# Holding back prefetch loads behind score blocks, and four x transposes by PE instead of DMA

## The chip, the cores and the metric

One core of a Trainium2 chip runs the whole kernel. The metric is the device time of one execution in microseconds (us); lower is better. Before the change it was 352.68 us (median of 3 runs, 351.48 to 353.09).

Engines, by what they do in this kernel: PE multiplies matrices, DVE (VectorE) and ACT (ScalarE) work on vectors, POOL issues the loads from device memory, SP issues the DMA transposes and the moves of v inside SBUF, where the kernel keeps its tiles. DMA engines carry out these transfers; the profile counts 16 of them for the core. PE's results go to PSUM (`ps` in the profile). The **landing** of a transfer is its time from issue to completion.

## The reference, cut to what matters

```python
# q, k, v: (8 batches, 8 heads, 576 positions, 64); window 64, causal
scores = q @ k^T / 8;  scores outside 0 <= i - j < 64 are masked
attn   = softmax(scores);  x = (attn @ v) as (4608 tokens, 512)
out    = (silu(x @ w_gate) * (x @ w_val)) @ w_out     # 512 -> 1536 -> 512
```

## The kernel before

The 4608 tokens are handled as 36 **chunks** n of 128 tokens (attention) and 9 **blocks** c of 512 tokens, four chunks each (feed-forward). The steps have these names:

- `load(n)`: POOL issues the loads of k, q and v of a chunk, float32 to bf16, into rings of 4 (k, q) and 10 (v) buffers.
- `T(n, "k")`, `T(n, "q")`: SP issues DMA transposes of k and q. `T8(n)` is both, and the shift of v by 64 rows (`shift_v`).
- `S(n)`: PE's scores, ACT's exponentials, DVE's mask. `AV(n)`: PE multiplies by v, DVE divides; the result is `xb`, 128 x 512 in bf16.
- `X(n)`: xb is transposed into `xT`, either by a DMA transpose from SP or by PE, with a copy out of PSUM. SP's lines in the traces stand in program order too, so an `X(n)` can stand behind a `T8` that waits for its load (chunk 11's x in the kernel before: ready at 83.75 us, issued at 85.94, behind T8(13)).
- `F(c, f)`: gate and value products of a block (8 matmuls), `O(c, u)`: output product (12 matmuls).

Each engine is given its own steps in program order. F(c, 0) needs the x of **all four** chunks of the block: F(2, 0) needs X(8) to X(11).

```python
    def load(self, n, what="kqv"):
        ...
                self.g.op("pool", lambda e, d=d, a=a: e.dma_start(d, a), writes=ks, dma=True)

    def T(self, n, x):                       # i = n % 4: the ring of k and q
        ...
        self.g.op("sp", lambda e: e.dma_start_transpose(d, src[:, :]), reads=[(x + "n", i, j) for j in range(2)],
                  writes=wk, dma=True)

    def X(self, n, eng="sp"):
        ...
        if eng == "sp":
            g.op("sp", lambda e: e.dma_start_transpose(xo, xb[:, :]), reads=xk, writes=[("xT", it, u)], dma=True)
            return
        bank, bk = self.bank("a")            # one of three PSUM banks, shared with S and AV
        ...                                  # 4 PE transposes, then a copy by eng ("act" or "dve")

    def build(self):
        ...
        for n in (8, 9, 10, 11):
            self.load(n)
        for n in (8, 9, 10):
            self.T8(n)
            self.load(n + 4)
        ...                                  # S, AV, X of 6 and 7; F(1, f) in halves
        F1(0, 1); self.O(0, 0); self.S(8)
        F1(2, 3); self.AV(8); self.X(8); self.T8(11); self.load(15)
        F1(4); self.O(0, 1); self.S(9)
        F1(5, 6); self.AV(9); self.X(9); self.T8(12); self.load(16)
        F1(7); self.S(10); self.O(0, 2); self.AV(10); self.X(10)
        self.F(1, 8); self.S(11); self.T8(13); self.load(17)
        self.F(1, 9); self.AV(11); self.X(11)
        self.F(1, 10); self.O(0, 3); self.S(12); self.T8(14); self.load(18)
        self.F(1, 11)
        for c in range(2, NFC):
            for u in range(4):
                n = 4 * c + u + 4
                self.F(c, 3 * u)
                self.AV(n)
                self.T(n + 3, "k")
                self.X(n)
                self.T(n + 3, "q")
                self.shift_v(n + 3)
                self.load(n + 7)
                self.F(c, 3 * u + 1)
                self.S(n + 1)
                ...                          # O(c - 1, u), F(c, 3 * u + 2)
```

(The calls of `build` are put several to a line here.)

The softmax here doesn't subtract the row's maximum and nothing guards it: scores larger than these inputs give would overflow.

Of the kernel before, what the change touches and what calls it, by code (L numbers as in the profile page):

```python
# [5 lines left out]
ALU = mybir.AluOpType  # L6

B, H, S, D = 8, 8, 576, 64
DM, DFF = H * D, 1536
T = B * S  # L10
# [139 lines left out]
class _Kernel:  # L150
# [70 lines left out]
    def segs(self, t0, size):  # L221
        r = 0
        while r < size:
            b, s = divmod(t0 + r, S)
            L = min(size - r, S - s)
            yield r, b, s, L
            r += L
# [44 lines left out]
            out=m[:, :], in_=m[:, :], compare_op=ALU.not_equal, fill=1.0, base=0,  # L272
            pattern=[[-1, 128]], channel_multiplier=1), writes=[key])

    def load(self, n, what="kqv"):
        if n >= NCH:
            return
        parts = list(self.segs(128 * n, 128))
        for x in what:
            src = {"k": self.k, "q": self.q, "v": self.v}[x]  # L280
            if x == "v":
                dst, nm, i = self.va[n % self.NV], "va", n % self.NV
            else:
                i = n % self.NQ
                dst = (self.kn if x == "k" else self.qn)[i][:, :].rearrange("p (h d) -> p h d", h=H)
                nm = x + "n"
            for j, (r, b, s, L) in enumerate(parts):
                d = dst[r:r + L, :, 0:64]
                a = src[b, :, s:s + L, :].rearrange("h p d -> p h d")
                ks = [(nm, i, j)] if len(parts) > 1 else [(nm, i, 0), (nm, i, 1)]  # L290
                self.g.op("pool", lambda e, d=d, a=a: e.dma_start(d, a), writes=ks, dma=True)  # L291

    def shift_v(self, n, eng="sp"):
        if n >= NCH:
# [48 lines left out]
    def S(self, n, bias=False):  # L343
        if n >= NCH:
            return
        g = self.g
        ip, iz = n % self.NP, n % self.NZ
        pt = self.pt[ip]
        bx = [self.bank("a"), self.bank("a")]
        sv = [b[0][:, :].rearrange("p (w c q) -> p w c q", w=2, c=4) for b in bx]  # L350
        nm = self.nmask[:, :].rearrange("p (a q) -> p a q", a=4)[:, self.var(n)]
        nm = nm.unsqueeze(2).to_broadcast([128, 2, 4, 64])

        def pe(e):
            if bias:
                for p in range(2):
                    e.matmul(sv[p], self.ident[:, :], nm, start=True, stop=False)  # L357
            for w in range(2):
                k0 = 128 * n + 64 * w
                for c in range(4):  # L360
                    for p in range(2):
                        ps = slice(64 * p, 64 * p + 64)
                        r = e.matmul(sv[p][:, w, c], self.kT[ps, c, k0:k0 + 128],  # L363
                                     self.qT[ps, c, self.qs(n, 64 * w, 64 * w + 64)],
                                     start=not bias, stop=not bias or (w == 1 and c == 3))
            return r

        rd = [("kT", m, b) for m in (n - 1, n) for b in range(2)] + [("qT", iz, b) for b in range(2)]
        rd += ["nmask", "ident"] if bias else []
        g.op("pe", pe, reads=rd, writes=[b[1] for b in bx])  # L370
        m = self.mask[:, :].rearrange("p (a q) -> p a q", a=4)[:, self.var(n)]
        m = m.unsqueeze(2).to_broadcast([128, 2, 4, 64])
        for p in range(2):
            po = pt[:, p::2, :].rearrange("p h (x q) -> p x h q", x=3)[:, 0:3:2]
            pk = ("pt", ip, p)
            g.op("act", lambda e, po=po, p=p: e.activation(po, sv[p], ACTF.Exp, scale=SCALE), reads=[bx[p][1]], writes=[pk])  # L376
            if not bias:
                g.op("dve", lambda e, po=po: e.tensor_tensor(po, po, m, ALU.mult), reads=[pk, "mask"], writes=[pk])  # L378
# [269 lines left out]
    def build(self):  # L648
        self.opening()
        self.Tpe(4, ("dve", "act"))  # L650
        self.F(0, 6)
        self.S(4)
        self.F(0, 7)
        self.AV(4)
        self.Tpe(5, ("dve", "act"))
        self.F(0, 8)
        self.X(4, "act")
        self.S(5)
        self.F(0, 9)
        self.AV(5)  # L660
        self.F(0, 10)
        self.X(5, "act")
        self.F(0, 11)
        self.Tpe(6, ("dve", "act"))
        self.Tpe(7, ("dve", "act"))
        for n in (8, 9, 10, 11):
            self.load(n)
        for n in (8, 9, 10):
            self.T8(n)
            self.load(n + 4)  # L670
        F1 = lambda *fs: [self.F(1, f, 0, 256) for f in fs]
        F1(0)
        self.S(6)
        F1(1, 2)
        self.AV(6)
        F1(3)
        self.S(7)
        F1(4)
        self.X(6, "act")
        F1(5)  # L680
        self.AV(7)
        F1(6, 7)
        self.X(7, "act")
        self.banks("a", [5, 6, 7])
        self.banks("o", [4])
        F1 = lambda *fs: [self.F(1, f, 256, 512) for f in fs]
        F1(0, 1)
        self.O(0, 0)
        self.S(8)
        F1(2, 3)  # L690
        self.AV(8)
        self.X(8)
        self.T8(11)
        self.load(15)
        F1(4)
        self.O(0, 1)
        self.S(9)
        F1(5, 6)
        self.AV(9)
        self.X(9)  # L700
        self.T8(12)
        self.load(16)
        F1(7)
        self.S(10)
        self.O(0, 2)
        self.AV(10)
        self.X(10)
        self.F(1, 8)
        self.S(11)
        self.T8(13)  # L710
        self.load(17)
        self.F(1, 9)
        self.AV(11)
        self.X(11)
        self.F(1, 10)
        self.O(0, 3)
        self.S(12)
        self.T8(14)
        self.load(18)
        self.F(1, 11)  # L720
        for c in range(2, NFC):
            for u in range(4):
# [4 lines that stand above are left out]
                self.X(n)  # L727
                self.T(n + 3, "q")
                self.shift_v(n + 3)
                self.load(n + 7)  # L730
                self.F(c, 3 * u + 1)
                self.S(n + 1)
                late = c == NFC - 1 and u == 3
                if not late:
                    self.O(c - 1, u)
                self.F(c, 3 * u + 2)
                if late:
                    self.O(c - 1, u)
        self.banks("o", [0, 1, 2, 3])
        for u in range(3):  # L740
            self.O(NFC - 1, u)
        self.O_last(NFC - 1, 3)
        self.g.emit()
# [42 lines left out]
```

## Time and profile before

| | before |
|---|---|
| time, median (range) | 352.68 us (351.48 to 353.09) |
| span of the profiled execution | 348.9 us (time 350.69) |
| PE busy | 330.9 us |
| PE gap before block 2 | 6.05 us, ends at 94.46 us |
| iteration in steady state | 8.70 us |

First, lines of the profile's page of the kernel before: the busy line, then rows of 40 slices of 8.7 us. A digit is tenths; PEclk is the clock granted to PE.

```profile
span 348.9 us, 6788 instructions
PE 330.9 (95%) x2689; PEld 171.5 (49%) x2689; DVE 222.5 (64%) x495; ACT 136.1 (39%) x248; POOL 111.3 (32%) x139
...
PE   7889998989399999999999999999999999999996
...
PEclk9999999999699999999999999999999999999999
DMA  9999999999999999999999999999934421100012
```

PE is full except in the opening and in one slice, the eleventh (87 to 96 us): busy 3, clock 6. The DMA engines are full from the start to about 250 us. A long row of nines says that transfers are under way nearly all the time, not that PE waits for them: from 100 to 250 us PE is busy for 150.00 of 150 us under them. What PE waits for is in the waits. Here they are for PE of the kernel before, 60 to 100 us (us in total, times, longest):

```profile
PE ps L500 <- issue: 6.0, 1, 6.0
PE ps L363 <- DVE uu L519: 1.2, 1, 1.2
PE ps L363 <- DVE xb L403: 0.7, 1, 0.7
```

"issue" means that the profile shows no releaser. The timeline says what came next. The PE lines of the kernel before around the gap (start, length, then idle time before it in brackets; L363 scores, L500 feed-forward; x4 or x16 is the number of matmuls in a line):

```profile
79.19 0.41 PE L363 MATMUL ps<-qT,kT 64*128 64x64 bf16 x16 [1.21 <-DVE uu L519]
...
87.39 1.03 PE L500 MATMUL ps<-xT,Wv 128*128 128x512 bf16 x4
94.46 1.86 PE L500 MATMUL ps<-xT,Wg 128*128 128x512 bf16 x4 [6.05 <-issue]
96.12 1.70 PE L500 MATMUL ps<-xT,Wv 128*128 128x512 bf16 x4
```

The group at 94.46 us is F(2, 0). Its x of chunk 11 was issued by SP at 85.94 us. And the group runs at about half speed: 1.66 us from start to start instead of 0.86, at a granted clock of 0.53 (94.46 to 97.70 us). The last view is the DMA issues of the kernel before between 60 and 95 us (count, KB each, median us from issue to landing):

```profile
qn<-in_q_dram POOLq DMA_DIRECT2D x5, 128.0 KB, 11.6
va<-in_v_dram POOLq DMA_DIRECT2D x5, 128.0 KB, 12.3
kn<-in_k_dram POOLq DMA_DIRECT2D x4, 128.0 KB, 10.7
...
kT<-kn SPq DMA_TRANSPOSE x6, 8.2
qT<-qn SPq DMA_TRANSPOSE x5, 9.1
xT<-xb SPq DMA_TRANSPOSE x4, 8.4
```

The x transpose of chunk 11, issued at 85.94 us, itself landed 8.4 us later, so at 94.3 us: that is PE's gap. Later in the same kernel (150 to 200 us) the same transpose lands in 4.1 us.

### The profile page before, as it was taken

The page shows a single profiled execution, that of the slowest core. Times are in us where ns is not written, and L with a number is a line of the kernel's source. Part 1 is how long each engine was busy: PE and PEld are TensorE (multiplying, and loading weights), DVE is VectorE, ACT ScalarE, POOL GpSimd, SP SyncE. Part 2 cuts the span into 40 slices and gives each one's busy share as a digit, 9 for nine tenths or more (in the row PEclk, how much of TensorE's full clock was granted, in tenths as well). Part 3 has the DMA queues.
Part 4 walks back from the last instruction along what each step waited for, and adds up shares of the span by engine and source line. Part 5 has one row for each costly group of instructions (what it writes and reads, how often), then busy time and mean ns, then how long its engine had stood idle before and what let it go on. Part 6 is the DMA issues. An engine that isn't in the chain of part 4 may idle for free.

```text
span 348.9 us, 6788 instructions
## 1 busy us (share of the span) xinstructions
PE 330.9 (95%) x2689; PEld 171.5 (49%) x2689; DVE 222.5 (64%) x495; ACT 136.1 (39%) x248; POOL 111.3 (32%) x139
## 2 busy tenths in 40 slices
PE   7889998989399999999999999999999999999996
PEld 3557575644144444444444444444444444444444
DVE  8788987475256666666666666666666666655520
ACT  3545463433134443333333333333333333232321
POOL 8999562634343334233233334232100000000000
PEclk9999999999699999999999999999999999999999
DMA  9999999999999999999999999999934421100012
GB/s 174 173 183 190 183 200 164 175 154 178 178 165 150 159 141 141 133 143 147 134 147 133 148 136 146 142 141 119 147 94 96 107 47 46 57 30 30 32 50 102
DMA packets 176543, 45.46 MB, mean 130 GB/s; under 512 B 160064, under 2 KB 172032, under 8 KB 176512
## 3 DMA queue, kind: packets, MB, share of 16 engines
q0 software_dynamic: 118368, 18.36, 77.5%
q1 hardware_dynamic: 51920, 16.84, 28.2%
q10 hardware_dynamic: 6224, 9.83, 8.1%
q8 instruction: 21, 0.34, 0.4%
q14 instruction: 10, 0.08, 0.1%
HBM read 37.75 MB, written 9.44 MB: 135 GB/s over the span
## 4 chain that ended last, share of the span: by engine, by line
PE 86%; DVE 6%; ACT 3%; issue 3%; DMA 1%; ACTq 0%
PE ps L500 49%; PE ps L546 27%; PE ps L363 3%; PE ps L393 2%; PE ps L394 2%; DVE uu L519 2%; ACT pt L376 2%; DMA hT<-in_k_dram 1%; DVE xb L403 1%; DVE hT L522 1%; PE ps L568 1%; ACT sig L511 1%; ACT ost L551 1%; PE ps L476 1%; PE ps L357 0%
## 5 line engine op out<-in xcount | busy, mean ns | idle before, releaser
L519 DVE SCALAR_TENSOR_TENSOR uu<-sig,ps 128x512 bf16<-128x512 bf16 (+1 forms) x122 | 75.9, 622 | 90.9 <-ACT sig L511 90.2
L500 PE MATMUL ps<-xT,Wg 128*128 128x512 bf16 (+1 forms) x488 | 114.3, 357 | 8.2 <-issue 6.0
L500 PE MATMUL ps<-xT,Wv 128*128 128x512 bf16 (+1 forms) x488 | 114.0, 356 | 0.2 <-DMA Wv<-in_moe_w_val_dram 0.2
L511 ACT ACTIVATE sig<-ps 128x512 bf16<-128x512 f32 (+1 forms) x122 | 66.8, 550 | 107.6 <-PE ps L500 107.5
L546 PE MATMUL ps<-Wo,hT 128*128 128x512 bf16 x420 | 96.1, 380 | 0.0
L522 DVE SCALAR_TENSOR_TENSOR hT<-uu,ps 128x512 bf16<-128x512 bf16 (+1 forms) x122 | 76.3, 625 | 4.4 <-PE ps L500 0.2
L500 PEld LDWEIGHTS ps<-xT,Wv 128*128 128x128 bf16 x488 | 47.5, 98 | 47.2 <-issue 1.1
L500 PEld LDWEIGHTS ps<-xT,Wg 128*128 128x128 bf16 x488 | 44.3, 98 | 47.3 <-issue 7.1
L546 PEld LDWEIGHTS ps<-Wo,hT 128*128 128x128 bf16 x420 | 39.1, 98 | 44.7
L291 POOL DMA_DIRECT2D qn<-in_q_dram x38 | 33.2, 878 | 79.6 <-DMA qT<-qn 79.5
L291 POOL DMA_DIRECT2D kn<-in_k_dram x38 | 33.3, 878 | 53.2 <-DMA kT<-kn 47.2
L376 ACT ACTIVATE pt<-ps 128x512 bf16<-128x512 f32 x72 | 39.0, 595 | 22.4 <-PE ps L363 21.2
L551 ACT ACTIVATE ost<-ps 128x512 f32<-128x512 f32 x35 | 20.9, 597 | 67.0 <-PE ps L546 67.0
L291 POOL DMA_DIRECT2D va<-in_v_dram x40 | 35.4, 890 | 0.2 <-issue 0.2
L403 DVE TENSOR_TENSOR xb<-ps,rc 128x256 bf16<-128x256 f32 x72 | 30.5, 424 | 2.5
L378 DVE TENSOR_TENSOR pt<-pt,mask 128x512 bf16<-128x512 bf16 x64 | 24.8, 419 | 10.1 <-ACT pt L376 9.6
L393 PE MATMUL ps<-vb,pt 128*128 128x65 bf16 x288 | 22.8, 193 | 0.1
L394 PE MATMUL ps<-va,pt 128*128 128x65 bf16 x288 | 22.9, 194 | 0.0
L393 PEld LDWEIGHTS ps<-vb,pt 128*128 128x128 bf16 x288 | 20.2, 98 | 4.5 <-DVE pt L378 0.9
L394 PEld LDWEIGHTS ps<-va,pt 128*128 128x128 bf16 x288 | 19.0, 97 | 3.4
L363 PEld LDWEIGHTS ps<-qT,kT 64*128 64x128 bf16 x576 | 10.4, 95 | 16.3 <-DVE rc L400 9.3
L363 PE MATMUL ps<-qT,kT 64*128 64x64 bf16 x576 | 14.7, 191 | 1.9 <-DVE uu L519 1.2
(47 smaller groups left out, 84.7 us busy)
## 6 DMA issues: line engine op xcount, KB each, us to landing
out_dram<-ost ACTq DMA_DIRECT2D x35, 256.0 KB, 2.9
vb<-va SPq DMA_DIRECT2D x63, 80.0 KB, 3.3
va<-in_v_dram POOLq DMA_DIRECT2D x32, 128.0 KB, 5.3
kn<-in_k_dram POOLq DMA_DIRECT2D x30, 128.0 KB, 5.5
qn<-in_q_dram POOLq DMA_DIRECT2D x30, 128.0 KB, 5.3
Wo<-in_moe_w_out_dram POOLq DMA_DIRECT2D x2, 768.0 KB, 15.2
Wg<-in_moe_w_gate_dram POOLq DMA_DIRECT2D x4, 256.0 KB, 7.3
Wv<-in_moe_w_val_dram POOLq DMA_DIRECT2D x4, 256.0 KB, 7.9
```

Source lines behind the costliest of these rows:

```text
L291: self.g.op("pool", lambda e, d=d, a=a: e.dma_start(d, a), writes=ks, dma=True)
L363: r = e.matmul(sv[p][:, w, c], self.kT[ps, c, k0:k0 + 128], self.qT[ps, c, self.qs(n, 64 * w, 64 * w + 64)], start=not bias, stop=not bias ...
L376: g.op("act", lambda e, po=po, p=p: e.activation(po, sv[p], ACTF.Exp, scale=SCALE), reads=[bx[p][1]], writes=[pk])
L378: g.op("dve", lambda e, po=po: e.tensor_tensor(po, po, m, ALU.mult), reads=[pk, "mask"], writes=[pk])
L393: e.matmul(av[:, j, :], pt[:, h, 0:128], vb[:, h, 0:65], start=True, stop=False)
L394: r = e.matmul(av[:, j, :], pt[:, h, 64:192], va[:, h, 0:65], start=False, stop=True)
L403: g.op("dve", lambda e, xo=xo, av=av, rb=rb: e.tensor_tensor(xo, av[:, :, 0:64], rb, ALU.mult), reads=[bk, ("rc", ir)], writes=[("xb", ix, ...
L500: r = e.matmul(bank[:, lo:hi], W[:, kk, f * 128:f * 128 + 128], xT[:, kk, lo:hi], start=(kk == 0), stop=(kk == NK - 1))
L511: self.g.op("act", lambda e: e.activation(sig[:, lo:hi], G[:, lo:hi], ACTF.Tanh, scale=0.5), reads=[gk], writes=[("sig", i)])
L519: g.op("dve", lambda e: e.scalar_tensor_tensor(uu[:, lo:hi], sig[:, lo:hi], 1.0, G[:, lo:hi], ALU.add, ALU.mult), reads=[("sig", i), gk], ...
L522: g.op("dve", lambda e: e.scalar_tensor_tensor(hT[:, f, lo:hi], uu[:, lo:hi], 0.5, V[:, lo:hi], ALU.mult, ALU.mult), reads=[("uu", i), vk] ...
L546: r = e.matmul(OB[:, :], hT[:, f, 128 * u:128 * u + 128], self.Wo[:, f, :], start=(f == 0), stop=(f == NF - 1))
```

## The change

The intent, as the code shows it: keep the early loads of later chunks off the DMA while block 2's x is being made, and keep that x off the DMA altogether.

1. Gate: `load(12)` and later wait for a score step, S(n - 4), or S(n - 5) from chunk 16 on. In the loop this also makes the load one chunk shallower: n + 6 after S(n + 1), instead of n + 7.
2. `T8(11)` moves forward, right behind T8(10).
3. X(8) to X(11) go by PE, with the copy by ACT.

```diff
-    def load(self, n, what="kqv"):
+    def load(self, n, what="kqv", after=None):
+        gate = [] if after is None else [("S", after)]
...
-                self.g.op("pool", lambda e, d=d, a=a: e.dma_start(d, a), writes=ks, dma=True)
+                self.g.op("pool", lambda e, d=d, a=a: e.dma_start(d, a), reads=gate, writes=ks, dma=True)
...                                    (S(n) also writes the key ("S", n))
-        for n in (8, 9, 10):
+        for n in (8, 9, 10, 11):
             self.T8(n)
-            self.load(n + 4)
...
         self.S(8)
+        self.load(12, after=8)
         F1(2, 3)
         self.AV(8)
-        self.X(8)
-        self.T8(11)
-        self.load(15)
         F1(4)
         self.O(0, 1)
+        self.X(8, "act")
         self.S(9)
+        self.load(13, after=9)
+        self.T8(12)
         F1(5, 6)
         self.AV(9)
-        self.X(9)
-        self.T8(12)
-        self.load(16)
         F1(7)
+        self.X(9, "act")
         self.S(10)
+        self.load(14, after=10)
+        self.T8(13)
         self.O(0, 2)
         self.AV(10)
-        self.X(10)
         self.F(1, 8)
+        self.X(10, "act")
         self.S(11)
-        self.T8(13)
-        self.load(17)
+        self.load(15, after=11)
         self.F(1, 9)
         self.AV(11)
-        self.X(11)
+        self.T8(14)
         self.F(1, 10)
+        self.X(11, "act")
+        self.S(12)
+        self.load(16, after=11)
+        self.load(17, after=12)
         self.O(0, 3)
-        self.S(12)
-        self.T8(14)
-        self.load(18)
...                                    (in the loop)
-                self.load(n + 7)
                 self.F(c, 3 * u + 1)
                 self.S(n + 1)
+                self.load(n + 6, after=n + 1)
```

More of the change, by code (lines that the diff above doesn't have):

```diff
@@ L369, in S @@
         rd += ["nmask", "ident"] if bias else []
-        g.op("pe", pe, reads=rd, writes=[b[1] for b in bx])
+        g.op("pe", pe, reads=rd, writes=[b[1] for b in bx] + [("S", n)])
         m = self.mask[:, :].rearrange("p (a q) -> p a q", a=4)[:, self.var(n)]
```

## The prediction

> **What bounds it now.** PE is busy 330.9 of 348.9 us. From about 100 us to 300 us the timeline repeats one 8.70 us iteration without a PE gap: three feed-forward blocks (1.73 us each), an output block (2.60), attention (about 0.9). The change can't shorten that. The loss to recover lies in 60 to 98 us:
>
> - The waits of PE show one gap of 6.05 us ending at 94.46 us, labelled "issue". The next matmul is the first feed-forward of token block 2, which needs the x of chunks 8 to 11. Chunk 11's x transpose was issued at 85.94 us, and this line's landings take 6.9 to 9.8 us (60 to 95 us), against about 4 later: about 94.4.
> - The two groups after it take 3.2 us instead of 1.73; granted clock 0.66 in 90 to 100 us. [...] Cost 1.5 us.
> - The scores of chunk 11 start 1.2 us late (79.19). By the pool queue's waits chunk 11's qT landed near there.
>
> All are long DMA landings: between 60 and 95 us the k, q, v loads land in 10 to 13 us (whole run: 5.3), the kT, qT, xT transposes in 8 to 9. [...] early loads of chunks 12 to 18 delay the urgent transposes.
>
> **What the change does.** It holds the loads to one chunk per score block, moves chunk 11's transposes ahead of them, and takes four x transposes off the DMA.
>
> Removed from the critical path: 6.05 + 1.5 + 1.2 = 8.8 us.
>
> Added to it: four PE transposes of x, 0.22 to 0.25 us each: 0.9 us. Each has an ACT copy (0.60 us) ahead of the next exponentials, and takes one of three attention PSUM banks; PE already waits 0.7 us for one at 72.67. I estimate 1.0 us of small new waits there.
>
> Steady state: a load is one chunk later, still over two iterations (17 us) ahead of use. But k, q and v now start together just as the x transpose is issued; before, usually only k met it, with landings of 3.6 to 4.6 us. The x of each block's last chunk has about 4.5 us until PE needs it (134.98 to 139.46). I allow 1 us in all for four such boundaries.
>
> Net: 8.8 - 0.9 - 1.0 - 1.0 = 5.9 us off the span, 343.0 us. The profiled run (350.69) is 2 us below the unprofiled median (352.68); part may be the same DMA wait, varying by run, so I subtract 7.5 from the median.
>
> **Prediction: 345.2 us, range 342.5 to 349.0.** Faster by over 2%: 0.54; within 2%: 0.44; slower: 0.02.
>
> **What would show it right.** The 6 us gap leaves PE's waits; no granted clock near 0.66 at 90 us; block 2's first feed-forward starts near 89 us; transposes land in about 4 us or less between 60 and 95 us; POOL waits on PE's scores instead of kT and qT; iterations stay 8.70 us.
>
> **What would make it wrong.** Gaps of 0.5 to 2 us before the first feed-forward of blocks 3 to 6 (late x, colliding with gated loads) would eat up to 6 us. Bank and ACT waits around AV(9) to AV(11) of over 2 us in sum. A gap only halved, because its cause is not DMA crowding.

The 1.5 us for the clock is read from the trace. That early loads delay the transposes was the author's estimate, from loads that landed in 10 to 13 us here against 5.3 over the whole run; e9 below tests it.

## The result, and the profile after

The kernel after took 343.75 us (median of 4 runs, 343.43 to 344.10) against 352.31 us of before (4 runs): ratio 0.9758, 95% interval 0.973 to 0.9785, faster by 2.4%. Ratios are the mean time of one kernel's fast runs over that of the other's in the same rounds, so not quite the ratio of the medians quoted. The profiled execution took 343.43 us, span 341.6 us.

The same lines of the page, of the kernel after:

```profile
span 341.6 us, 6841 instructions
PE 330.3 (97%) x2705; PEld 172.2 (50%) x2705; DVE 222.5 (65%) x495; ACT 138.3 (40%) x252; POOL 111.8 (33%) x139
...
PE   7889998989999999999999999999999999999996
...
PEclk9999999999999999999999999999999999999999
```

The hole in PE and the slow clock are gone. PE's waits of the kernel after, 60 to 100 us, and PE's lines where block 2 begins (at 88.66 us), with the one larger wait that is new (L423 is the PE transpose of x, here chunk 9's):

```profile
PE ps L423 <- DVE xb L404: 1.6, 2, 1.3
PE ps L394 <- DVE pt L379: 0.2, 1, 0.2
```

```profile
73.09 0.40 PE L423 MATMUL ps<-ident,xb 128*128 128x128 bf16 x4 [1.28 <-DVE xb L404]
...
87.80 1.03 PE L501 MATMUL ps<-xT,Wv 128*128 128x512 bf16 x4
88.66 1.03 PE L501 MATMUL ps<-xT,Wg 128*128 128x512 bf16 x4
```

The surprise is in the DMA issues of the kernel after, 60 to 95 us:

```profile
kn<-in_k_dram POOLq DMA_DIRECT2D x6, 128.0 KB, 7.1
qn<-in_q_dram POOLq DMA_DIRECT2D x6, 128.0 KB, 7.5
va<-in_v_dram POOLq DMA_DIRECT2D x5, 128.0 KB, 8.7
...
kT<-kn SPq DMA_TRANSPOSE x6, 6.9
qT<-qn SPq DMA_TRANSPOSE x6, 6.3
xT<-xb SPq DMA_TRANSPOSE x1, 3.8
```

The k and q transposes are faster than before (8.2 and 9.1 us), but far from the 4 us that the prediction gave as its sign, and the loads still take 7.1 to 8.7 us (before: 10.7 to 12.3). The gate has not made this stretch quiet: between 60 and 95 us the kernel after moves 6.55 MB by DMA, before 6.01 MB. (In part that is because after is further along at 95 us; from 60 to 86 us it is 4.88 against 4.42 MB.) The gate moves loads around but a deep prefetch has to be filled by about 90 us all the same; chunks 15, 16 and 17 are issued in one go from 79.8 to 87.7 us. So which part of the change made the gap go?

### The profile page after: what moved, and what is told of

It is laid out like the page before. It is cut to its first block, busy times and chain, and to the rows that moved or that the text cites. A ratio compares the mean times of both kernels' runs of the same rounds, so it can differ in the third digit from the quotient of the medians.

```text
span 341.6 us, 6841 instructions
## 1 busy us (share of the span) xinstructions
PE 330.3 (97%) x2705; PEld 172.2 (50%) x2705; DVE 222.5 (65%) x495; ACT 138.3 (40%) x252; POOL 111.8 (33%) x139
## 4 chain that ended last, share of the span: by engine, by line
PE 86%; DVE 4%; POOL 3%; ACT 2%; DMA 2%; issue 1%; ACTq 0%; POOLq 0%
PE ps L501 50%; PE ps L547 27%; PE ps L364 3%; PE ps L394 2%; PE ps L395 2%; DMA Wv<-in_moe_w_val_dram 2%; DVE uu L520 2%; ACT pt L377 1%; POOL va L292 1%; DVE xb L404 1%; DVE hT L523 1%; PE ps L569 1%; POOL Wg L317 1%; PE ps L423 1%; POOL qn L292 1%
```

## The experiments

Two theories. **A**, as in the prediction: the early loads crowd the DMA, and the gate takes the crowd away. **B**: the crowd stays, and what helps is that block 2's x does not travel by DMA any more. In the diffs, "after" or "before" says which kernel was edited.

### e1: the gate without PE's transposes

```diff
 (after) X(8) to X(11), each moved right behind its AV(n)
-        self.X(n, "act")
+        self.X(n)
```

> The kernel after with one part undone: the x of chunks 8 to 11 goes by DMA again, right behind AV of its chunk; gated loads and early transposes of chunk 11 stay. Theory A (early loads crowd the DMA, and the gate alone cures it): x landings between 60 and 95 us fall from 8.4 us to about 4, no PE gap over 1 us before the first feed-forward of block 2, time 342.5 to 344.5 us, no slower than after. Theory B (after moves as many load bytes between 60 and 95 us as before, 6.55 MB in all against 6.01; what helps is that the x leaves the DMA): x landings 6 to 8 us, a gap of 1.5 to 4 us before block 2, time 345.5 to 349 us.

Measured: 349.44 us (347.43 to 351.41; ratio 0.9928, 0.9895 to 0.9961). One line each from PE's waits and from the DMA issues of 60 to 95 us of this kernel:

```profile
PE ps L501 <- DMA xT<-xb: 6.9, 1, 6.9
```

```profile
xT<-xb SPq DMA_TRANSPOSE x4, 9.0
```

Theory A falls. With gated loads the x transposes land in 9.0 us, no better than before, and the profile now names the DMA as the releaser of a 6.9 us gap. The numbers lie even beyond theory B's ranges (landings of 6 to 8 us, a gap of at most 4 us, 349 us). The profiled run, 351.28 us, is at the slow end of this kernel's own, but all six have a mean granted clock of 0.984 to 0.995, as before has (0.985 to 0.990), while the kernels without the gap have 0.998 to 1.000; so a slowed clock is left in every run of e1. The gate and the early T8(11) alone are worth 3.0 us in the medians; the profiled run doesn't show where, since its span (349.5 us) is no shorter than the 348.9 of before.

One caution: e1 has another order on SP than before. X(10) was ready at 76.55 us and issued at 82.52, behind T8(13), which waited for its gated load. X(11), which PE waits for, lost only 2.2 us so (ready at 81.80, issued at 84.03), as in before.

### e2: PE's transposes without the gate

```diff
 (before) X(8) to X(11), at the places that they have in after
-        self.X(n)
+        self.X(n, "act")
```

> The kernel before with the other part alone: the x of chunks 8 to 11 by PE, loads and k, q transposes where they were. Theory A: the crowding stays, kT and qT of chunks 11 and 12 land late (8 to 9 us), so the scores of 11 and 12 wait 1 to 2 us each and some more comes in the next iterations: 345.5 to 348 us. Theory B: the 6 us gap and the slow clock after it are gone, nothing else changes: 343.5 to 345.5 us.

Measured: 344.70 us (343.55 to 345.03; ratio 0.9784, 0.9761 to 0.9806). That is 7.7 us less than before (352.43 in these rounds), from the x alone. Block 2 starts at 88.69 us, as in after. Chunk 11's scores don't wait either, although T8(11) is at its old place in the program: with X(8) off SP's queue, SP issues the k transpose of chunk 11 at 64.33 us instead of 67.84. So taking x off SP also lets the other transposes go earlier; the runs don't separate the two. Theory B holds. But a small gap is new, before F(3, 0), the first group of block 3; the PE line of this kernel:

```profile
124.41 1.02 PE L500 MATMUL ps<-xT,Wg 128*128 128x512 bf16 x4 [0.73 <-DVE uu L519]
```

### e3: only the last x by PE

```diff
 (before) X(11) moved behind F(1, 10)
-        self.X(11)
+        self.X(11, "act")
```

> The kernel before with the x of chunk 11 alone by PE; 8 to 10 stay on the DMA. Theory B in its narrow form (only the last x of the block has no slack): the gap before block 2 is gone, three PE transposes and their waits for AV(9) less than in after: 342.5 to 345 us. If the x of chunk 10, landing 7 to 10 us after about 79.3 us, becomes the next late one, a gap of 0 to 1.5 us is left. Theory A: about as e2, 345.5 to 348 us.

Measured: 346.54 us (345.36 to 347.21; ratio 0.9838, 0.9814 to 0.9861): above theory B's range (342.5 to 345), and in fact in the range given to theory A. The trace decides: the gap before block 2 is gone, one transpose buys it, and what is lost is elsewhere. Chunk 11's scores wait 1.29 us as before, and the gap before block 3 is larger:

```profile
124.76 1.02 PE L500 MATMUL ps<-xT,Wg 128*128 128x512 bf16 x4 [1.47 <-DVE hT L522]
```

I had not expected this second gap. The kernel before doesn't show it. Measured: take the first gap away, and PE reaches block 3 some 6 us earlier (124.8 instead of 130.75 us); the x of chunk 15, issued at 118.7 us, lands in 6.0 us, where in the kernel before it was issued at 126.28 and landed in 3.7. That the DMA caught up in before while PE stood still for 6 us, and is still behind here, is my estimate from these landings; no trace shows it directly.

### e4: the gate in the opening only

```diff
 (after)
+        self.load(18, after=12)
...                                    (in the loop)
+                self.load(n + 7)
-                self.load(n + 6, after=n + 1)
```

> The kernel after with the gate taken out of the steady loop only (load of chunk n+7 in its old place). Both theories: the steady part is bound by PE, so no change in time: within 0.5 us of after (343.2 to 344.3 us), iterations 8.70 us; x landings in the loop go back from 2.7 to about 4 us without cost. If the gate in the loop did matter, 345 us or more, with gaps before the first feed-forward of blocks 3 to 8.

Measured: 344.27 us (343.55 to 344.79; ratio 0.9776, 0.9755 to 0.9796). Within the range, near its upper end. Its trace has a gap of 0.20 us before block 3; x lands in 4.7 us (100 to 150 us) instead of after's 2.8.

The profile puts these gaps down to DVE or to "issue", but their size follows the landing of chunk 15's x, issued between 118.7 and 119.7 us in all of these traces. PE needs it 4.5 to 4.6 us after its issue; what the landing takes beyond that is the gap, within 0.1 us:

| kernel | landing of chunk 15's x, us | gap before block 3, us |
|---|---|---|
| after | 3.2 | none |
| e4, loop not gated | 4.8 | 0.20 |
| e10 (below) | 4.9 | 0.36 |
| e2, no gate | 5.3 | 0.73 |
| e3, no gate, only X(11) by PE | 6.0 | 1.47 |

Once the x transposes have taken the first gap away, the gate's worth lies here: a gap of 0.7 us, about 1 us between the medians of after and e2 (whose ratios have overlapping intervals).

### e5: gated loads, fewer of them

```diff
 (e1)
-        self.load(15, after=11)
-        self.load(16, after=11)
-        self.load(17, after=12)
+        self.load(15, after=12)
...                                    (in the loop)
-                self.load(n + 6, after=n + 1)
+                self.load(n + 4, after=n + 1)
```

> The x of 8 to 11 by DMA and gated loads, as in e1_gate_xdma, but the loads of 15, 16, 17 and later come later (n+4 instead of n+6), so that only chunks 12 to 15 instead of 12 to 17 load between 60 and 90 us. If load bytes crowd the DMA: the x of chunks 10 and 11 land in 4 to 6 us instead of 9, the gap before block 2 falls from 6.9 to 1.5 to 3.5 us, time 345 to 347.5 us. If the sync engine's own queue of transposes and moves makes them late, the landings stay at 8 to 9 us and the time at 348.5 to 350.5 us.

Measured: 346.23 us as the median of four runs that fall in two groups: 344.49 and 344.50, 347.94 and 348.13 (ratio 0.9806, 0.975 to 0.9862). The profiled run is of the slower group: x landings 7.7 to 9.2 us, gap 4.16 us. The direction fits crowding, but the landings of chunks 10 and 11 (7.7 us) do not reach the 4 to 6 us expected. The two faster runs have a mean clock of 1.000, the two slower 0.995. The traced kernels without a gap before block 2 have 0.998 to 1.000 in all runs, the traced slower run of e5 had the 4.16 us gap; so my estimate is that with fewer loads the gap shrinks in some executions. The faster two were not traced. On its own this run is inconclusive; e9 was made to settle it.

### e9: no loads at all in that stretch (wrong result)

```diff
 (before) def load
-        if n >= NCH:
+        if n >= NCH or 12 <= n <= 18:
```

> The kernel before without the loads of chunks 12 to 18: their tiles keep older data, so the result is wrong on purpose; every other instruction and its order stay, x by DMA. It takes the suspected crowd away whole. If load bytes make the x transposes late: x landings between 68 and 95 us fall from 8.4 us to 2.3 to 4 us, chunk 11's scores don't wait, the gap before block 2 is 0 to 1 us, time 343 to 345 us. If the transposes and moves of the sync engine's own queue are the cause: landings of 7 us or more, gap over 4 us, 348 us or more.

Measured: 343.14 us (342.02 to 344.95; ratio 0.973, 0.9682 to 0.9778), result wrong as intended. The profiled run took 342.02 us, so the spread of the others is not traced. DMA issues of this kernel, 68 to 95 us:

```profile
kT<-kn SPq DMA_TRANSPOSE x5, 2.5
qT<-qn SPq DMA_TRANSPOSE x5, 3.9
xT<-xb SPq DMA_TRANSPOSE x4, 2.4
```

With the loads away, the same x transposes, on the same queue and in the same order, land in 2.4 us, and PE has no gap before block 2. SP's order alone is not the cause: here too X(11) was issued 1.8 us after its xb was complete. So the loads are the crowd; that half of theory A was right. What was wrong is that this gate thins the crowd enough.

### e8: the kernel before, once more

> The kernel before once more, for its trace: is the gap before block 2 longer in an execution nearer the median? If the 2 us between the profiled run (350.69) and the median (352.4) are this DMA wait, the gap is 7 to 8 us instead of 6.05 at a time of 352 to 353 us; if not, the gap is again 6 us and the time differs elsewhere.

Measured: 351.95 us, a single run, so of unknown state; used for its trace alone. The first two of PE's waits of this execution, 60 to 100 us:

```profile
PE ps L500 <- issue: 7.0, 1, 7.0
PE ps L363 <- DMA qT<-qn: 1.8, 1, 1.8
```

The gap is 7.0 us instead of 6.05, and the wait of chunk 11's scores is 1.8 us instead of 1.2. Together that is some 1.5 us more. The span is 1.2 us longer although the opening was 0.6 us shorter (56.12 against 56.73 us), so most of what this run takes longer is these DMA waits. The second line also corrects a label: in the first trace the same wait was put down to DVE; here the profile names the DMA, as the prediction had argued. The first trace agrees: its qT of chunk 11, issued at 69.15 us, landed 10.0 us later, when the scores started (79.19).

### e10: the loop's gate without the shallower prefetch

```diff
 (e2) load and S with the gate as in after; in the loop
-                self.load(n + 7)
...
                 self.S(n + 1)
+                self.load(n + 7, after=n + 1)
```

> The x of chunks 8 to 11 by PE and old loads as in e2_loads_old_xpe, and only the loop's loads gated (chunk n+7 behind the scores of n+1, so behind the x transpose instead of around it). If what the gate gives is the order in the loop: x landings in the loop 2.4 to 3.5 us instead of 3.8 to 4.9, no gap before block 3 (0.73 us in e2), 343.4 to 344.3 us, as after. If the gate's worth lies in the loads of 12 to 17 being held back: as e2, 344.5 to 345 us, with the gap.

Measured: 345.20 us (343.72 to 345.84; ratio 0.9779, 0.9744 to 0.9814), no better than e2; x lands in 4.7 and 4.1 us (100 to 150, 150 to 200 us). My expectation was wrong: the order "x first, then the load" is not enough. The POOL lines and the x lines of SP in this kernel, one iteration:

```profile
155.68 0.87 POOL L292 DMA_DIRECT2D kn<-in_k_dram  x1 [1.40 <-PE ps L364]
161.22 0.87 POOL L292 DMA_DIRECT2D qn<-in_q_dram  x1 [4.67 <-DMA qT<-qn]
162.08 0.88 POOL L292 DMA_DIRECT2D va<-in_v_dram  x1
```

```profile
163.69 1.19 SPq L416 DMA_TRANSPOSE xT<-xb  x1
```

and the same in the kernel after:

```profile
154.52 0.88 POOL L292 DMA_DIRECT2D kn<-in_k_dram  x1 [6.08 <-PE ps L364]
155.39 0.88 POOL L292 DMA_DIRECT2D qn<-in_q_dram  x1
156.25 0.89 POOL L292 DMA_DIRECT2D va<-in_v_dram  x1
```

```profile
153.83 1.19 SPq L416 DMA_TRANSPOSE xT<-xb  x1
...
162.53 1.19 SPq L416 DMA_TRANSPOSE xT<-xb  x1
```

At depth n + 7 the buffer of q is the one that T(n + 3, "q") is still reading, so q (and v behind it on POOL) wait for that transpose and start 1.6 to 2.5 us **before the next x**. At depth n + 6 the buffer is already free: k, q and v start together, 0.7 us behind one x and over 6 us ahead of the next. Then the x finds the DMA free: for 1.1 us after its issues at 153.83, 162.53 and 171.24 us the DMA row of after reads 0 (in before it reads 9 after 152.39 and 161.09 us, 0 to 8 after 169.79), and it lands in 2.7 us (150 to 200 us) instead of e10's 4.1. Depth n + 6 without the gate was not run; whether the gate is needed too stays open.

### e6 and e7: looking for something better

After spends four PE transposes where e3 says that only the last ones are late. e6 sends X(8) and X(9) by DMA again:

```diff
 (after) n = 8 and 9, each moved right behind its AV(n)
-        self.X(n, "act")
+        self.X(n)
```

> The kernel after with the x of chunks 8 and 9 by DMA again, 10 and 11 still by PE. They have over 12 us until block 2, more than any landing seen (10 us), so no gap comes back; two PE transposes and the 1.3 us wait of the x of chunk 9 go (0.7 us of the bank wait comes back). By the timeline of e1_gate_xdma, which starts the scores of chunk 10 1.4 us earlier than after: 342.0 to 342.9 us. If the x of chunk 9 lands late or delays the kT of chunk 13 behind it: 343.5 us or more.

Measured: 343.02 us (342.38 to 343.06; ratio 0.9727, 0.9705 to 0.9749). That is 0.1 us above the expected range, and better than after's 343.75. e7 also changes PE's order between 70 and 88 us:

```diff
 (e6)
-        S(10)  O(0,2)  AV(10)  F(1,8)  X(10)  S(11)  F(1,9)  AV(11)  F(1,10)  X(11)  S(12)  O(0,3)  F(1,11)
+        O(0,2)  S(10)  F(1,8)  AV(10)  F(1,9)  X(10)  S(11)  F(1,10)  AV(11)  F(1,11)  X(11)  S(12)  O(0,3)
```

> As e6_x8_x9_dma, with PE's order changed between 70 and 88 us: output block 0,2 goes before the scores of chunk 10, and each later AV, x transpose and score has one feed-forward more between it and what it waits for. This fills the bank wait of about 0.9 us before the scores of chunk 10 and the 0.3 us before the x of chunk 11: 0.7 to 1.3 us less than e6, 341.0 to 342.0 us. If another wait takes its place (VectorE or ScalarE behind), equal to e6.

Measured: 343.21 us (342.59 to 343.28; ratio 0.9733, 0.9711 to 0.9755): no gain. The bank wait before S(10) went, but AV(10), X(10) and X(11) now wait instead; from the same point of the opening (56.78 and 56.10 us), block 2 starts after 31.19 us in e6 and after 31.38 us in e7.

### e11 and e12: after and e6 on one chip

> The kernel after once more, for a comparison on one chip with e12: 343.4 to 344.1 us.

> The same kernel as e6_x8_x9_dma, on the same chip and rounds as e11: 342.4 to 343.1 us. If the difference to after is real, 0.5 to 1.2 us lower; the timelines differ by 1.36 us up to block 2's start, less the opening's 0.67 us of chance.

Measured in the same rounds: after 344.03 us (343.48 to 344.11; ratio 0.9748), e6's kernel 343.03 us (342.99 to 343.09; ratio 0.9722). The two ranges do not touch: 1.0 us, 0.3%. It is small, but real, and this version beats both kernels. In the traces PE reaches the last output group 1.33 us earlier; 0.4 us of that is lost between there and the end of the span, which I did not trace.

After's runs also come in two levels, near 343.45 and 344.05 us. The traces put that into the opening, before anything that the change touches: the same feed-forward group starts at 56.10 us in the profiled run of 343.43 us and at 56.74 us in that of 344.02 us.

## Why the prediction was right or wrong

The number was right: 345.2 us predicted, range 342.5 to 349.0, measured 343.75. "Faster by over 2%" had 0.54, and it came. Here is the sum term by term, for the two profiled spans. The measured waits are what is left of block 2's earlier start (5.17 us from the same opening point) after the other terms.

| term of the prediction | predicted, us | measured, us | read from |
|---|---|---|---|
| gap before block 2 | -6.05 | -6.05 | waits |
| slow clock after it | -1.5 | -1.5 | 254.44 to 252.94 us from block 2's start to the end |
| scores of chunk 11 | -1.2 | -1.2 | waits |
| four PE transposes | +0.9 | +0.9 | 0.22 to 0.23 us each |
| bank and ACT waits | +1.0 | +1.2 | remainder; the largest, before X(9), is 1.28 against 0.73 |
| x late at later blocks | +1.0 | 0 | no PE gap after 88 us |
| opening | 0 | -0.6 | chance: 56.73 to 56.10 us |
| sum | -5.9 | -7.3 | 348.9 to 341.6 us |

Point by point:

- **Where the loss was: right.** One x landing late, and the clock behind it. After the gap of 6.05 us the next two groups took 3.2 us instead of 1.73 (granted clock 0.53 from 94.46 to 97.70 us); after e3's 1.47 us gap the clock stayed (the profile's 1.02 us for the next group is that of any other). Between the two, e5's 4.16 us was followed by a slowed clock as well (1.20 us instead of 0.86 from start to start of the next two groups, 0.83 granted from 90 to 100 us). From what length on a gap slows the clock was not shown.
- **That loads crowd the DMA: right,** shown by e9: 2.4 us without the loads, 8.4 us with them. Queue q0 moved 12,597 packets (1.58 MB) between 68 and 95 us of before, and 347 (0.04 MB) of e9. By which mechanism the loads hold up a transpose was not shown.
- **That the gate removes the crowd: wrong.** The prediction's sign "transposes land in about 4 us or less between 60 and 95 us" failed: kT and qT took 6.9 and 6.3 us in after, and x by DMA took 9.0 us in e1. (Its other signs came: no gap, no slow clock, block 2 at 88.66 us, POOL waiting for PE's scores.) The gap went because x left the DMA (e2: -7.7 us; e1: -3.0 us; both together -8.6 us in their own rounds). The prediction listed both parts and never asked which one carried the term, so the sum came out right all the same; that part is luck.
- **"k, q and v now start together just as the x transpose is issued": right as a fact, wrong in sign.** This is the term that failed. I charged 1.0 us for the collision. Measured, x landed in 2.7 us instead of 4.1 (150 to 200 us), and no boundary waited. A burst right behind one x is out of the way of the next. Without the gated, shallower loads there would have been a cost of 0.2 to 1.5 us before block 3 (e2, e3, e4).
- **Subtracting more from the median than from the span: right in direction.** The medians differ by 8.6 us, the spans by 7.3; e8 shows a longer DMA wait (7.0 us instead of 6.05) in a run nearer the median.
- **Steady iterations of 8.70 us: right.** In after, the scores of chunks 13 and 14 start at 92.70 and 101.41 us, 8.71 us apart.

One alternative was not run: sending the x transposes from ACT's DMA queue while SP's transposes run. What it would do to the time or to the result is not shown here.

## What to carry to other kernels

When a PE-bound kernel has one long gap, find the single transfer that ended it and ask whether it must be a transfer at all: here 0.23 us of PE and a 0.60 us copy by ACT replaced an 8 us DMA landing, with the loads as they were (e2). Holding loads back did not speed up this x in e1, where as many bytes fell into the stretch as before (6.09 against 6.01 MB); it helped later, where the loads fell at a better moment. So check the bytes and the landings of a stretch, not the intent of the gate. And look for the next gap behind the one removed: here PE came to block 3 some 6 us earlier, and the next x was late there (e2, e3).
